# Pooled attention with a one-expert router on one core: batch 1's choice of expert, buffer counts, the first batch's order and the last batch's output blocks

## The chip, the cores and the metric

The kernel runs on one NeuronCore of a Trainium2 chip. The metric is the device time of one execution in microseconds (us), as the median of several. Engines are named as the profile has them: PE is TensorE's matmuls and PEld its weight loads, DVE is VectorE, ACT is ScalarE, POOL is GpSimd, and SP is the engine that issues the stores of the output. An L with a number is a line of the kernel before.

## The reference, cut to what matters

Attention over keys and values pooled by 8, then a cosine router that sends each token to one of eight experts, then that expert's two matmuls.

```python
# attention: q, k, v are [8 batches, 8 heads, 576 tokens, 64]
k_p = k.reshape(B, H, S // 8, 8, D).mean(axis=3)      # 72 pooled keys
v_p = v.reshape(B, H, S // 8, 8, D).mean(axis=3)
attn = softmax(q @ k_p.T / sqrt(D))
x = (attn @ v_p)                                      # as [4608 tokens, 512]
# router and experts: expert_emb [8, 512], w1 [8, 512, 1024], w2 [8, 1024, 512]
logits = normalized(x) @ normalized(expert_emb).T / tau
expert_idx = argmax(logits, axis=1)
gate_w = softmax(logits)[arange(N), expert_idx]
for e in range(8):
    mask = expert_idx == e
    h = maximum(x[mask] @ w1[e], 0)
    out[mask] = gate_w[mask, None] * (h @ w2[e])
```

## The kernel before

Work is staged by batch, 576 tokens each, in four blocks of 128 tokens and a short one of 64. Attention of batch b pools k and v (`pool_kv`, L185, matmuls in L151), transposes q (`qtr`, L192) and the pooled keys (`kpt`, L204), computes each head's scores and their exp (`score`, L219, exp on ACT in L236, one `at` tile of 16 buffers each), multiplies with the pooled values (`pv`, L240, one call a block; DVE divides into `x_sb`, L256 and L258), and transposes x (`xtr`, L263; the copy to `xt_all` is DVE, L276 and L278). `route` (L285) computes router logits, their maximum and a one-hot row per token; `count` (L308) sums these rows over the tokens, and `expert` (L315) takes the most frequent expert, reads its number into a register of POOL and has POOL issue the loads of its weights (`load_w`, L90, three buffers). In batch 0 the choice is made from block 0 alone, the other blocks are routed later, and `recount` (L336) records which experts occur in the whole batch. In the other batches all five blocks are routed and counted ahead of the choice. A loop at the kernel's end (L639) makes a further pass for every pair of a batch and an occurring expert that wasn't the chosen one.

The expert's part (`ffn_steps`, L430) has eight `hgrp` steps (eight W1 matmuls each, L442, with a ReLU on ACT in even steps, L449, and on DVE in odd ones, L451), eight `yblk` steps (four W2 matmuls each, L460; blocks 0 and 1, then 2 and 3, share a PSUM tile and are evicted together with the gate factor, the even one on DVE, L472, the odd one on ACT, L470) and `ylast` (L476) for the short block, evicted half by DVE (L488) and half by ACT (L490). Each block goes to a `y_sb` tile (four buffers, L66), and SP issues its two stores (L515). Where two engines read one PSUM tile, the second starts when the first is done. All PSUM tiles come from one ring of four (L67).

Every engine works in the order in which the program emits its instructions, and that order is written out by hand. Each step has a cost, and a step's place in its batch is its share of the summed costs. The main loop (L614) emits the expert steps of batch b and, ahead of each, all attention and gate steps whose place lies below `lead` (L610) of it: some 1.5 to 1.7 batches ahead. The gate steps of `gate_steps` (L396: `norm`, a power on POOL; `prob`, three DVE operations and an exp on ACT; `gate`, five DVE operations) have places of their own (L607).

```python
# attn_steps, b == 0: the head of the first batch (L349 to L362)
step(0.65)(lambda h=h: score(h, (12, 4, 4, 4, 10, 4, 4, 4)[h]))
# main: the rest of batch 0, interleaved with the first steps of batch 1 (L601)
for f in [s1[0], tail[0], s1[1], tail[1], tail[2], s1[2], s1[3], tail[3],
          tail[4], s1[4], tail[5], tail[6], s1[5], tail[7], s1[6], tail[8],
          s1[7], tail[9]]:
    f()
```

In the first batch nothing else is there for TensorE, and `fill` (L129) puts matmuls on a constant between the steps; their number is the second argument of `score`, `xtr`, `route` and `expert`. `head` is emitted first, then `tail` (here `pv(1)` and on) interleaved with the first eight steps of batch 1 (`s1`). The inputs come by POOL's queue: batch 0 in pieces (L530 to L544), batch 1 at L576, batch 2 at the end of the head, and batch b + 2 right after the choice of batch b (L341, L393); `kv` and `qq` have three buffers.

Of the kernel before, what the change touches and what calls it, by code (L numbers as in the profile page):

```python
# [27 lines left out]
def kernel(  # L28
# [30 lines left out]
    wpool = ctx.enter_context(tc.tile_pool(name="wpool", bufs=3))  # L59
    inp = ctx.enter_context(tc.tile_pool(name="inp", bufs=3))  # L60
    att = ctx.enter_context(tc.tile_pool(name="att", bufs=2))
    atp = ctx.enter_context(tc.tile_pool(name="atp", bufs=16))
    xp = ctx.enter_context(tc.tile_pool(name="xp", bufs=3))
    rt = ctx.enter_context(tc.tile_pool(name="rt", bufs=2))
    hp_ = ctx.enter_context(tc.tile_pool(name="hp", bufs=2))
    yp = ctx.enter_context(tc.tile_pool(name="yp", bufs=4))  # L66
    ps = ctx.enter_context(tc.tile_pool(name="ps", bufs=4, space=bass.MemoryType.PSUM))  # L67

    def psum():
# [66 lines left out]
    def attn_steps(b):  # L136
# [178 lines left out]
        def expert(cs, nfill=0):  # L315

            pc = psum()
            fill(pc[:, 512:704], nfill)
            count(cs, pc)
            mx = rt.tile([128, E], FP32, name="mx")  # L320
            nc.vector.max(out=mx, in_=pc[:, 0:E])
            ix = rt.tile([1, E], U32, name="ix")
            nc.vector.max_index(out=ix, in_max=mx[0:1], in_values=pc[0:1, 0:E])
            nc.vector.tensor_scalar(out=eb_all[:, b], in0=pc[:, 0:E], scalar1=mx[:, 0:1],
                                    scalar2=None, op0=ALU.is_ge)
            if len(cs) == NC:
                present(pc)
            e_val = nc.values_load(ix[0:1, 0:1], engines=[ENG.Pool], min_val=0,
                                   max_val=E - 1)
            weights[b] = load_w(e_val)  # L330

        def present(pc):
            nc.vector.tensor_scalar(out=pos_all[:, b], in0=pc[0:1, 0:E], scalar1=0.5,
                                    scalar2=None, op0=ALU.is_ge)

# [2 lines left out]
            count(list(range(NC)), pc)  # L338
            present(pc)

        def next_load():  # L341
            if b + 2 < B:
                load_qkv(b + 2)

        routes[b] = st
        P = lambda c: step(0.9)(lambda: pv(c))
        X = lambda c: step(0.6 if c < 4 else 1.2)(lambda: xtr(c))
        if b == 0:
            for grp in range(2):  # L349
                step(0.5)(lambda grp=grp: pool_k(grp))  # L350
                step(0.5)(lambda grp=grp: qtr(grp))
                step(0.5)(lambda grp=grp: kpt(2 * grp, 2))
                for h in range(4 * grp, 4 * grp + 4):
                    step(0.65)(lambda h=h: score(h, (12, 4, 4, 4, 10, 4, 4, 4)[h]))
                    if h == 5:
                        step(1.0)(pool_v)
            step(0.3)(lambda: emb_transposed(8))
            P(0)
            step(0.6)(lambda: xtr(0, 14))
            step(0.4)(lambda: route(0, 1, 8))  # L360
            step(0.4)(lambda: expert([0], 12))
            step(0.0)(lambda: load_qkv(2))  # L362
            head, steps = steps, []
            P(1)
            P(2)
            X(1)
            P(3)
            X(2)
            P(4)
            X(3)  # L370
            X(4)
            step(0.8)(lambda: route(1, 4))
            step(0.4)(recount)
            return head, steps
# [7 lines left out]
        P(1)  # L382
        X(0)
        P(2)
        X(1)
        P(3)
        X(2)
        P(4)
        X(3)
        X(4)  # L390
        step(1.0)(lambda: route(0, NC))
        step(0.4)(lambda: expert(list(range(NC))))
        step(0.0)(next_load)  # L393
        return steps

    def gate_steps(b):  # L396
# [30 lines left out]
        return [norm, prob, gate]  # L427


    def ffn_steps(xt, get_w, get_gm, finish):  # L430
        st = {}
        steps = []

# [19 lines left out]

        def yblk(c, part):
            w2 = get_w()[1]
            if part == 0 and c % 2 == 0:
                st['y'] = psum()
            py = st['y'][:, ts(c % 2, 512)]
            for w in range(4 * part, 4 * part + 4):
                nc.tensor.matmul(out=py,  # L460
                                 lhsT=st['hT'][:, w // 2, w % 2, ts(c, 128)],
                                 rhs=w2[:, w // 2, w % 2, :],
                                 start=(w == 0), stop=(w == 7))
            if part == 1 and c % 2:
                for i in (c - 1, c):
                    y_sb = yp.tile([128, DM], FP32, name="y_sb")
                    py = st['y'][:, ts(i % 2, 512)]
                    g = get_gm()[:, i:i + 1]
                    if i % 2:
                        nc.scalar.activation(out=y_sb, in_=py, func=AF.Copy, scale=g)  # L470
                    else:
                        nc.vector.tensor_scalar(out=y_sb, in0=py, scalar1=g, scalar2=None,  # L472
                                                op0=ALU.mult)
                    finish(i, y_sb)

        def ylast():  # L476
            w2 = get_w()[1]
# [15 lines left out]

        for w in range(8):
            steps.append((1.0, lambda w=w: hgrp(w)))
        for c in range(4):
            for part in range(2):
                steps.append((0.87, lambda c=c, part=part: yblk(c, part)))
        steps.append((0.87, ylast))
        return steps  # L500

    def out_rows(o_b, c, y_sb):
# [7 lines left out]
    def store(b):  # L510
        o_b = out[ts(b, S)]

        def finish(c, y_sb):
            for dst, src in out_rows(o_b, c, y_sb):
                nc.sync.dma_start(out=dst, in_=src)  # L515
        return finish


# [9 lines left out]
    with tc.manual_schedule():  # L528
# [61 lines left out]
        for b in range(B):  # L590
# [7 lines left out]
            if b == 1:  # L598

                s1 = [f for _, f in astream]  # L600
                for f in [s1[0], tail[0], s1[1], tail[1], tail[2], s1[2], s1[3], tail[3],  # L601
                          tail[4], s1[4], tail[5], tail[6], s1[5], tail[7], s1[6], tail[8],
                          s1[7], tail[9]]:
                    f()
                astream = astream[8:]
            for i, f in enumerate(gate_steps(b)):
                gstream.append((b + LEAD + 0.05 + 0.12 * i, f))  # L607
        astream = sorted(astream + gstream, key=lambda s: s[0])

        def lead(pos):  # L610
            return pos + LEAD - 0.2 * max(0.0, 1.0 - pos)

        j = 0
        for b in range(B):  # L614
            steps = ffn_steps(lambda b=b: xt_all[:, b], lambda b=b: weights[b],
                              lambda b=b: gates[b], store(b))
            total = sum(c for c, _ in steps)
            done = 0.0
            for c, f in steps:
                while j < len(astream) and astream[j][0] < lead(b + done / total):  # L620
                    astream[j][1]()
                    j += 1
                f()
                done += c
# [14 lines left out]
    with tc.For_i(0, n_val, 1) as i:  # L639
        f_val = nc.values_load(ext_i[0:1, ds(i, 1)], min_val=0, max_val=1)  # L640
        with tc.If(f_val > 0):
            b_val = nc.values_load(pair_b[0:1, ds(i, 1)], min_val=0, max_val=B - 1)
            e_val = nc.values_load(pair_e[0:1, ds(i, 1)], min_val=0, max_val=E - 1)
            wx = load_w(e_val)
            xt_c = att.tile([128, 4, S], FP16, name="xt_c", bufs=1)
            nc.vector.tensor_copy(
                out=xt_c, in_=xt_all[:, ds(b_val, 1), :, 0:S].squeeze(1))
            gmx = rt.tile([128, NC], FP32, name="gm")
# [6 lines left out]
            o_b = out[ds(b_val * S, S)]  # L655

            def finish(c, y_sb):
                o_sb = yp.tile([128, DM], FP32, name="o_sb", bufs=1)
                cols = DM if c < 4 else DM // 2
                for src, dst in out_rows(o_b, c, o_sb):  # L660
                    nc.sync.dma_start(out=dst, in_=src)
# [42 lines left out]
```

## Time and profile before

| what | before |
|---|---|
| median of 3 runs | 247.66 us (246.61 to 249.81) |
| profiled execution, its own time | 246.23 us |
| its span, first to last instruction | 244.6 us |
| PE busy | 218.2 us (89%) |
| PEld busy | 140.7 us (58%) |
| DVE busy | 128.1 us (52%) |
| ACT busy | 108.9 us (45%) |
| POOL busy | 42.9 us (18%) |
| mean granted TensorE clock | 0.965 of full speed |
| bytes moved by DMA, mean rate | 40.79 MB, 167 GB/s |

The span lies within the execution's own time, and 1.6 us are around it. Busy time of PE is that of pipelined matmuls whose ends are modelled: an engine that is shown as busy is not always at its peak. The granted clock has two levels here, full (1.00, 2.4 GHz) and half (0.50, 1.2 GHz). The DMA share of a window can pass 1.

### The profile page before, as it was taken

The page shows a single profiled execution, that of the slowest core. Times are in us where ns is not written, and L with a number is a line of the kernel's source. Part 1 is how long each engine was busy: PE and PEld are TensorE (multiplying, and loading weights), DVE is VectorE, ACT ScalarE, POOL GpSimd, SP SyncE. Part 2 cuts the span into 40 slices and gives each one's busy share as a digit, 9 for nine tenths or more (in the row PEclk, how much of TensorE's full clock was granted, in tenths as well). Part 3 has the DMA queues.
Part 4 walks back from the last instruction along what each step waited for, and adds up shares of the span by engine and source line. Part 5 has one row for each costly group of instructions (what it writes and reads, how often), then busy time and mean ns, then how long its engine had stood idle before and what let it go on. Part 6 is the DMA issues. An engine that isn't in the chain of part 4 may idle for free. (4 is left out here: it accounts for less than half of the span.)

```text
span 244.6 us, 5695 instructions
## 1 busy us (share of the span) xinstructions
PE 218.2 (89%) x2282; PEld 140.7 (58%) x2283; DVE 128.1 (52%) x370; ACT 108.9 (45%) x230; POOL 42.9 (18%) x61
## 2 busy tenths in 40 slices
PE   7799789999898996999899998999899999996940
PEld 2578557763676455664677366745666478465520
DVE  3224756852784356761786258535766288216220
ACT  3442483518273535537362647353553664214210
POOL 7400610070006100070007000530012000300000
PEclk9999957999999999999999999999999999999995
DMA  5996699659998999489995999599969941896061
GB/s 77 199 207 104 115 211 207 107 81 205 222 250 138 211 203 258 97 152 209 228 239 90 211 215 258 96 205 196 266 132 175 228 104 34 148 210 181 3 154 46
DMA packets 27597, 40.79 MB, mean 167 GB/s; under 512 B 1960, under 2 KB 15272, under 8 KB 27568
## 3 DMA queue, kind: packets, MB, share of 16 engines
q0 software_dynamic: 21152, 30.94, 73.2%
q1 hardware_dynamic: 6416, 9.46, 13.0%
q8 instruction: 19, 0.31, 0.5%
q14 instruction: 10, 0.08, 0.1%
HBM read 61.88 MB, written 9.44 MB: 292 GB/s over the span
## 5 line engine op out<-in xcount | busy, mean ns | idle before, releaser
L442 PE MATMUL pa<-xt_all,w 128*128 128x288 f16 x512 | 72.7, 290 | 2.6 <-ACT y_sb L490 2.5
L460 PE MATMUL pa<-w,hT 128*128 128x512 f16 x256 | 62.9, 380 | 0.0
L442 PEld LDWEIGHTS <-w 128*128 128x128 f16 x512 | 47.4, 99 | 17.0 <-issue 5.3
L236 ACT ACTIVATE at<-pa 72x576 f16<-72x576 f32 x64 | 38.1, 643 | 26.0 <-PE pa L230 25.8
L460 PEld LDWEIGHTS <-hT 128*128 128x128 f16 x256 | 21.9, 98 | 25.5 <-issue 5.6
L93 POOL DMA_DIRECT2D w<-in_moe_w_dram x8 | 6.3, 791 | 160.5 <-DVE vpx L169 121.9
L449 ACT ACTIVATE hT<-pa 128x576 f16<-128x576 f32 x32 | 20.7, 651 | 28.2 <-PE pa L442 28.0
L258 DVE TENSOR_TENSOR x_sb<-pa,r 128x512 f16<-128x512 f32 x40 | 27.7, 692 | 2.6
L472 DVE TENSOR_SCALAR y_sb<-pa,gm 128x512 f32<-128x512 f32 x16 | 12.0, 751 | 32.4 <-PE pa L460 32.4
L470 ACT ACTIVATE y_sb<-pa,gm 128x512 f32<-128x512 f32 x16 | 11.0, 688 | 37.4 <-DVE y_sb L472 37.4
L451 DVE TENSOR_SCALAR hT<-pa 128x576 f16<-128x576 f32 x32 | 24.1, 754 | 5.7 <-PE pa L442 5.4
L282 ACT ACTIVATE sq<-x_sb 128x512 f16<-128x512 f16 x40 | 25.0, 625 | 4.5 <-DVE x_sb L258 4.1
L249 PE MATMUL pa<-vpx,at 72*128 72x65 f16 (+1 forms) x384 | 19.2, 199 | 2.9 <-ACT at L236 1.2
L249 PEld LDWEIGHTS <-at 72*128 72x128 f16 (+1 forms) x384 | 16.3, 105 | 9.3 <-issue 3.0
L271 PE MATMUL pa<-ident_h,x_sb 128*128 128x128 f16 (+1 forms) x160 | 14.7, 217 | 6.8 <-DVE xt_all L276 4.9
L151 PE MATMUL pa<-kv,pmat 64*72 64x512 f16 (+2 forms) x180 | 17.5, 336 | 0.7 <-DMA kv<-in_v_dram 0.7
L230 PE MATMUL pa<-qT,kpT 64*72 64x320 f16 (+1 forms) x128 | 17.0, 316 | 0.7 <-ACT at L236 0.2
L271 PEld LDWEIGHTS <-x_sb 128*128 128x128 f16 (+1 forms) x160 | 10.6, 98 | 12.0 <-issue 7.1
L256 DVE RECIPROCAL r<-pa 128x8 f32<-128x8 f32 x40 | 8.1, 202 | 17.8 <-PE pa L249 17.7
L201 DVE COPY qT<-pa 128x1152 f16<-128x1152 f16 x16 | 12.0, 752 | 9.1 <-PE pa L199 9.1
L276 DVE COPY xt_all<-pa 128x512 f16<-128x512 f16 x32 | 13.3, 415 | 2.2 <-PE pa L271 2.0
L230 PEld LDWEIGHTS <-kpT 64*72 64x72 f16 x128 | 5.7, 112 | 12.8 <-issue 9.8
(95 smaller groups left out, 196.8 us busy)
## 6 DMA issues: line engine op xcount, KB each, us to landing
w<-in_moe_w_dram POOLq DMA_DIRECT2D x16, 1024.0 KB, 10.6
out_dram<-y_sb SPq DMA_DIRECT2D x64, 128.0 KB, 6.0
kv<-in_v_dram POOLq DMA_DIRECT2D x8, 576.0 KB, 19.4
kv<-in_k_dram POOLq DMA_DIRECT2D x7, 576.0 KB, 16.6
qq<-in_q_dram POOLq DMA_DIRECT2D x7, 576.0 KB, 23.0
out_dram<-y_sb SPq DMA_DIRECT2D x16, 64.0 KB, 5.6
kv<-in_k_dram POOLq DMA_DIRECT2D x2, 288.0 KB, 4.9
qq<-in_q_dram POOLq DMA_DIRECT2D x2, 288.0 KB, 5.7
```

What stands on the lines that cost most here:

```text
L151: nc.tensor.matmul(out=pk[0:G, par * 512 + c0:par * 512 + c0 + na * nh * D], lhsT=pmat[rows, t, :], rhs=kv[rows, a0:a0 + na, h0:h0 + nh, t ...
L230: nc.tensor.matmul(out=pS[0:G, c0:c0 + nb * 64].rearrange("g (t p) -> g t p", p=64), lhsT=st['kpT', h, half], rhs=qT[rows, blk, ts(h2, 64) ...
L236: nc.scalar.activation(out=at, in_=pS[0:G, 512 - 320:512 + 256], func=AF.Exp, scale=escale)
L249: nc.tensor.matmul(out=px[rows, h * 128:h * 128 + D + 1], lhsT=st['at', h][:, c * 128:c * 128 + L], rhs=st['vpx'][:, h // 2, h % 2, :], st ...
L258: nc.vector.tensor_tensor(out=x_sb, in0=pxv[:, :, 0:D], in1=r.unsqueeze(2).to_broadcast([128, H, D]), op=ALU.mult)
L271: nc.tensor.transpose(out=pt[:, w * 128:w * 128 + L], in_=xf[0:L, ts(w, 128)], identity=ident_h[:L, :L])
L276: nc.vector.tensor_copy(out=xt_all[:, b, :, ts(c, 128)], in_=ptv)
L282: nc.scalar.activation(out=sq, in_=xf, func=AF.Square, accum_out=st['ssq'][:, c:c + 1])
L442: nc.tensor.matmul(out=ph[:, half * 512:half * 512 + HALF], lhsT=w1v[:, kk, w // 2, w % 2, :], rhs=xt()[:, kk, ts(half, HALF)], start=(kk ...
L449: nc.scalar.activation(out=dst, in_=src, func=AF.Relu)
L451: nc.vector.tensor_scalar(out=dst, in0=src, scalar1=0.0, scalar2=None, op0=ALU.max)
L460: nc.tensor.matmul(out=py, lhsT=st['hT'][:, w // 2, w % 2, ts(c, 128)], rhs=w2[:, w // 2, w % 2, :], start=(w == 0), stop=(w == 7))
```

## The change

Batch 1, too, chooses its expert from block 0 alone: `route(0, 1)` and `expert([0])` stand between its x blocks, the other blocks are routed afterwards, and `recount` follows. The loads of batch b + 2 are issued in `expert` itself. `y_sb` has eight buffers instead of four, and `at` twelve instead of sixteen. The head of the first batch is a new list: the second pair of key heads is pooled between the scores of the first heads, most steps have fewer fills, and `pv(1)` comes ahead of the choice; `xtr(1)` gets six fills. The list that interleaves batches 0 and 1 has one entry less. `norm` gets the place b + 1.0, `prob` b + 1.82 for b + 1.87, and `gate` b + 1.94 for b + 1.99. The new expression of `lead` has the same values as the old one at every place. In the last batch (`apart`) the short block comes ahead of the other blocks, each of these has a PSUM tile and an eviction of its own, and the second of each block's two stores is issued by ACT instead of SP. The loop at the end takes its tiles from other pools.

```diff
-    atp = ctx.enter_context(tc.tile_pool(name="atp", bufs=16))
+    atp = ctx.enter_context(tc.tile_pool(name="atp", bufs=12))
-    yp = ctx.enter_context(tc.tile_pool(name="yp", bufs=4))
+    yp = ctx.enter_context(tc.tile_pool(name="yp", bufs=8))
...
             weights[b] = load_w(e_val)
+            if b + 2 < B:
+                load_qkv(b + 2)
...
         if b == 0:
-            for grp in range(2):
-                step(0.5)(lambda grp=grp: pool_k(grp))
-                step(0.5)(lambda grp=grp: qtr(grp))
-                step(0.5)(lambda grp=grp: kpt(2 * grp, 2))
-                for h in range(4 * grp, 4 * grp + 4):
-                    step(0.65)(lambda h=h: score(h, (12, 4, 4, 4, 10, 4, 4, 4)[h]))
-                    if h == 5:
-                        step(1.0)(pool_v)
-            step(0.3)(lambda: emb_transposed(8))
-            P(0)
-            step(0.6)(lambda: xtr(0, 14))
-            step(0.4)(lambda: route(0, 1, 8))
-            step(0.4)(lambda: expert([0], 12))
-            step(0.0)(lambda: load_qkv(2))
+            for f in [lambda: pool_k(0), lambda: qtr(0), lambda: kpt(0, 2),
+                      lambda: score(0, 12), lambda: score(1, 2), lambda: pool_k(1),
+                      lambda: score(2, 2), lambda: qtr(1), lambda: score(3),
+                      lambda: kpt(2, 2), lambda: score(4, 4), lambda: score(5, 4),
+                      lambda: pool_v(), lambda: score(6, 2), lambda: score(7, 4),
+                      lambda: emb_transposed(6), lambda: pv(0), lambda: xtr(0, 14),
+                      lambda: route(0, 1, 8), lambda: pv(1), lambda: expert([0], 8)]:
+                step(1.0)(f)
             head, steps = steps, []
-            P(1)
             P(2)
-            X(1)
+            step(0.6)(lambda: xtr(1, 6))
...
         P(2)
+        if b == 1:
+            step(0.3)(lambda: route(0, 1))
         X(1)
+        if b == 1:
+            step(0.3)(lambda: expert([0]))
...
-        step(1.0)(lambda: route(0, NC))
-        step(0.4)(lambda: expert(list(range(NC))))
-        step(0.0)(next_load)
+        if b == 1:
+            step(0.8)(lambda: route(1, 4))
+            step(0.3)(recount)
+        else:
+            step(1.0)(lambda: route(0, NC))
+            step(0.4)(lambda: expert(list(range(NC))))
...
-            if part == 0 and c % 2 == 0:
+            if part == 0 and (apart or c % 2 == 0):
                 st['y'] = psum()
...
-            if part == 1 and c % 2:
-                for i in (c - 1, c):
+            if part == 0 or (c % 2 == 0 and not apart):
+                return
+            for i in ((c,) if apart else (c - 1, c)):
...
+        steps += [(0.87, ylast)] + ysteps if apart else ysteps + [(0.87, ylast)]
...
-                nc.sync.dma_start(out=dst, in_=src)
+            for i, (dst, src) in enumerate(out_rows(o_b, c, y_sb)):
+                (nc.scalar if b == B - 1 and i else nc.sync).dma_start(out=dst, in_=src)
...
-                for f in [s1[0], tail[0], s1[1], tail[1], tail[2], s1[2], s1[3], tail[3],
-                          tail[4], s1[4], tail[5], tail[6], s1[5], tail[7], s1[6], tail[8],
-                          s1[7], tail[9]]:
+                for f in [s1[0], tail[0], s1[1], tail[1], s1[2], s1[3], tail[2],
+                          tail[3], s1[4], tail[4], tail[5], s1[5], tail[6], s1[6], tail[7],
+                          s1[7], tail[8]]:
...
-                gstream.append((b + LEAD + 0.05 + 0.12 * i, f))
+                gstream.append((b + (1.0, LEAD + 0.12, LEAD + 0.24)[i], f))
```

## Rows read from the trace of the kernel before

**Rows 1.** The page: TensorE's clock in 40 slices, and the W1 matmuls' group

```profile
PEclk9999957999999999999999999999999999999995
...
L442 PE MATMUL pa<-xt_all,w 128*128 128x288 f16 x512 | 72.7, 290 | 2.6 <-ACT y_sb L490 2.5
```

**Rows 2.** Windows, one batch: length, busy us of PE, PEld, DVE, ACT, POOL; clock, DMA share, GB/s

```profile
171.89:198.34 26.45, 25.09 (x271) 16.01 (x269) 15.42 (x44) 13.27 (x29) 2.76 (x3) 1.00 0.90 184
```

**Rows 3.** Waits over the span: us in total, times, longest us

```profile
DVE y_sb L488 <- DMA out_dram<-y_sb: 7.6, 3, 4.7
...
PE pa L271 <- DVE xt_all L276: 4.9, 5, 1.6
PE pa L442 <- ACT y_sb L490: 2.5, 1, 2.5
...
PE pa L151 <- DMA kv<-in_v_dram: 0.7, 1, 0.7
```

**Rows 4.** Timeline, batch 1's short block: start, length, engine; idle time before and its releaser

```profile
87.13 1.33 SPq L515 DMA_DIRECT2D out_dram<-y_sb  x1
...
92.27 1.14 PE L442 MATMUL pa<-xt_all,w 128*128 128x288 f16 x8
...
94.45 0.48 DVE L488 TENSOR_SCALAR y_sb<-pa,gm 64x256 f32<-64x256 f32 x1 [1.87 <-DMA out_dram<-y_sb]
...
95.31 0.38 PE L271 MATMUL pa<-ident_h,x_sb 128*128 128x128 f16 x4 [1.64 <-DVE xt_all L276]
...
95.54 1.14 PE L442 MATMUL pa<-xt_all,w 128*128 128x288 f16 x8
```

**Rows 5.** DMA issues at 87.1 to 87.2: KB each, us from issue to landing

```profile
out_dram<-y_sb SPq DMA_DIRECT2D x1, 128.0 KB, 7.2
```

**Rows 6.** Timeline, batch 5's short block: two W1 groups in a row

```profile
198.34 1.14 PE L442 MATMUL pa<-xt_all,w 128*128 128x288 f16 x8
...
199.80 1.14 PE L442 MATMUL pa<-xt_all,w 128*128 128x288 f16 x8
```

**Rows 7.** DMA issues at 105.3 to 106: v of batch 5

```profile
kv<-in_v_dram POOLq DMA_DIRECT2D x1, 576.0 KB, 20.5
```

**Rows 8.** Timeline: the issue of that load, and its first reader

```profile
105.69 0.77 POOL L87 DMA_DIRECT2D kv<-in_v_dram  x1
...
127.90 1.27 PE L151 MATMUL pa<-kv,pmat 64*72 64x512 f16 x10
```

**Rows 9.** Timeline, batch 3's third W1 group, last x block and `prob` (L405)

```profile
124.07 0.69 DVE L258 TENSOR_TENSOR x_sb<-pa,r 128x512 f16<-128x512 f32 x1
...
124.84 0.65 ACT L449 ACTIVATE hT<-pa 128x576 f16<-128x576 f32 x1 [1.01 <-PE pa L442]
...
125.74 0.16 DVE L405 TENSOR_SCALAR rn<-ssq 128x5 f32<-128x5 f32 x1
...
126.17 0.18 PE L289 MATMUL pa<-tie_l,ones_m 128*128 128x40 f16 x1
```

**Rows 10.** Timeline in the first batch: fourteen fills, and batch 0's first W1 group

```profile
19.55 1.32 PE L132 MATMUL pa<-ones_m 128*128 128x192 f16 x14
...
36.48 2.11 PE L442 MATMUL pa<-xt_all,w 128*128 128x288 f16 x8
```

**Rows 11.** Windows in the first batch, columns as in rows 2

```profile
25.00:30.00 5.00, 3.59 (x62) 2.80 (x61) 4.15 (x9) 2.13 (x6) 3.71 (x5) 0.95 0.73 116
35.00:40.00 5.00, 4.67 (x38) 3.11 (x37) 2.02 (x7) 2.64 (x6) 0.51 (x1) 0.52 1.17 209
```

**Rows 12.** Timeline, the end: last matmuls, last large eviction on ACT, last store

```profile
234.03 1.06 PE L482 MATMUL pa<-w,hT 128*64 128x256 f16 x16
...
234.97 0.69 ACT L470 ACTIVATE y_sb<-pa,gm 128x512 f32<-128x512 f32 x1 [2.82 <-DVE y_sb L472]
...
238.96 0.55 SPq L515 DMA_DIRECT2D out_dram<-y_sb  x1
```

**Rows 13.** DMA issues at 231.4 to 231.9: the first store of the last batch

```profile
out_dram<-y_sb SPq DMA_DIRECT2D x1, 128.0 KB, 2.2
```

More of the change, by code (lines that the diff above doesn't have):

```diff
@@ L339, in recount @@
             present(pc)
-        def next_load():
-            if b + 2 < B:
-                load_qkv(b + 2)
         routes[b] = st
@@ L427, in gate_steps, with ffn_steps @@
         return [norm, prob, gate]
-    def ffn_steps(xt, get_w, get_gm, finish):
+    def ffn_steps(xt, get_w, get_gm, finish, apart=False):
         st = {}
@@ L463, in yblk @@
                                  start=(w == 0), stop=(w == 7))
-            if part == 1 and c % 2:
-                for i in (c - 1, c):
[L466 to L474, printed above, removed]
+            if part == 0 or (c % 2 == 0 and not apart):
+                return
+            for i in ((c,) if apart else (c - 1, c)):
+                y_sb = yp.tile([128, DM], FP32, name="y_sb")
+                py = st['y'][:, ts(i % 2, 512)]
+                g = get_gm()[:, i:i + 1]
+                if i % 2:
+                    nc.scalar.activation(out=y_sb, in_=py, func=AF.Copy, scale=g)
+                else:
+                    nc.vector.tensor_scalar(out=y_sb, in0=py, scalar1=g, scalar2=None,
+                                            op0=ALU.mult)
+                finish(i, y_sb)
         def ylast():
@@ L495, in ffn_steps @@
             steps.append((1.0, lambda w=w: hgrp(w)))
[L496 to L499, printed above, removed]
+        ysteps = [(0.87, lambda c=c, part=part: yblk(c, part))
+                  for c in range(4) for part in range(2)]
+        steps += [(0.87, ylast)] + ysteps if apart else ysteps + [(0.87, ylast)]
         return steps
@@ L513, in finish @@
         def finish(c, y_sb):
-            for dst, src in out_rows(o_b, c, y_sb):
-                nc.sync.dma_start(out=dst, in_=src)
+            for i, (dst, src) in enumerate(out_rows(o_b, c, y_sb)):
+                (nc.scalar if b == B - 1 and i else nc.sync).dma_start(out=dst, in_=src)
         return finish
@@ L606 @@
             for i, f in enumerate(gate_steps(b)):
-                gstream.append((b + LEAD + 0.05 + 0.12 * i, f))
+                gstream.append((b + (1.0, LEAD + 0.12, LEAD + 0.24)[i], f))
         astream = sorted(astream + gstream, key=lambda s: s[0])
         def lead(pos):
-            return pos + LEAD - 0.2 * max(0.0, 1.0 - pos)
+            return pos + min(1.5 + 0.2 * pos, LEAD)
         j = 0
@@ L615 @@
             steps = ffn_steps(lambda b=b: xt_all[:, b], lambda b=b: weights[b],
-                              lambda b=b: gates[b], store(b))
+                              lambda b=b: gates[b], store(b), b == B - 1)
             total = sum(c for c, _ in steps)
@@ L644 @@
             wx = load_w(e_val)
-            xt_c = att.tile([128, 4, S], FP16, name="xt_c", bufs=1)
+            xt_c = inp.tile([128, 2, HP, T * D], FP16, name="kv")[:, 0]
             nc.vector.tensor_copy(
@@ L657, in finish @@
             def finish(c, y_sb):
-                o_sb = yp.tile([128, DM], FP32, name="o_sb", bufs=1)
+                o_sb = yp.tile([128, DM], FP32, name="y_sb")
                 cols = DM if c < 4 else DM // 2
```

## The prediction, written before the kernel was changed

> **What bounds the kernel now.** I read the page first: by the table above TensorE is busy for 218.2 of 244.6 us, and the next, VectorE, for 52%; the row of TensorE's clock shows one dent inside the run, in the sixth and seventh of 40 slices [rows 1]. So only time in which TensorE stands still, or runs slowly, can be won. A window cut from one batch's first W1 matmul to the next one's comes second: it lasts 26.45 us and holds 25.09 us of TensorE work at full clock [rows 2]. Something over a microsecond is lost once a batch. The list of waits names it [rows 3]: `DVE y_sb L488 <- DMA out_dram` (7.6 us, 3 times), and behind them TensorE itself, 4.9 us in five waits for `xt_all` and 2.5 us in one for L490. The timeline shows the chain [rows 4]: L488, the eviction of half of a batch's fifth output block, stands in VectorE's order ahead of the copy of a transposed x block. VectorE idles 1.87 us before it, and it starts at 94.45. The store issued at 87.13 [rows 4] took 7.2 us to land [rows 5], at 94.33: with four `y_sb` buffers the fifth block takes the first one's and waits for its store. TensorE's next transpose then waits 1.64 us for VectorE. The control is in the same trace: when the loads are over, the same piece runs without a wait, and W1 group follows W1 group in 1.46 us (198.34 to 199.80) where it took 3.27 us (92.27 to 95.54) [rows 4, 6].
>
> **Eight output buffers.** A block then takes the buffer of eight blocks earlier, well over a batch old: no store is that late. TensorE's waits of 4.9 and 2.5 us go [rows 3]. The ends of matmuls are modelled, so an interval shrinks by a little more than its idle time: in the batch shown by 3.27 - 1.46 = 1.81 us against 1.64. With 0.17 us more for each of five, 4.9 + 0.85 + 2.5 = 8.2 us. Bounds: 0 if something else holds L488, and 8.2. What is late next is the loads. The v of batch 5 is issued at 105.69 and takes 20.5 us [rows 7, 8], so it is there at 126.2, and its reader starts at 127.90 [rows 8]: 1.7 us of slack, of which about 1 us goes with the wait. It holds, narrowly. I take 8.2.
>
> **Twelve score buffers for sixteen.** A score tile then takes one of the batch before (or of the one before that), whose last reader, the `pv` of its last block, stands ahead of it in TensorE's own order. Cost 0; were it wrong, up to one x block's chain a batch, under a microsecond.
>
> **Gate steps earlier.** `prob` moves from behind batch b+1's last transposes to ahead of the third W1 group, and so ahead of that group's ReLU in ScalarE's order. In the trace x_sb ends at 124.76, the ReLU runs from 124.84, `prob` on VectorE only from 125.74, and TensorE asks for the ReLU's PSUM buffer with the router's matmuls at 126.17 [rows 9]. In the new order `prob`'s three VectorE operations (0.2 us each) run at 124.76 to 125.36; its exp (0.3) then stands before the ReLU (0.65), which ends near 126.35. The router waits 0.2 us. Six batches at 0.2 us are 1.2 us lost; bounds 0 (the exp finds room) and 6 x 0.65 = 3.9 (a whole ReLU). I take 1.2. `norm` earlier on POOL stays between the same two groups of loads, cost 0. `gate`, now ahead of the expert's count, delays the next weights by 0.2 to 0.6 us, free while the slack above lasts. `load_qkv` inside `expert` keeps its place in POOL's order, 0.
>
> **Batch 1's expert from 128 tokens.** It adds one router pass and one count: three VectorE operations and three small matmuls, about 0.6 us, and puts the choice's four operations (another 0.6) ahead of batch 1's later x blocks. In return W(1) and the inputs of batch 3 are asked for several W1 groups sooner, so the one wait of TensorE for such a load, 0.7 us [rows 3], goes. The added 1.2 us are counted with the first batch.
>
> **First batch.** There are 22 fewer fill matmuls before batch 1's pooling (66 for 88); 14 of them took 1.32 us [rows 10], so 2.1 us; `pv(1)` moves in, 0.4 us. Part of the fills only stood in waits for exps, so I take 1.3 us for the head (0 to 1.7). Then comes the interleave of two batches. Here VectorE is nearly full (4.15 of 5 us) and TensorE is not (3.59), and the granted clock falls to 0.5, the lower of its two levels, 1.2 GHz; it rises again near 39.8 (0.52 for 35 to 40) [rows 11]. `pv(1)`'s two VectorE operations (0.9 us) leave this stretch for one where VectorE has room. So 1.3 + 0.9 - 1.2 = 1.0 us. The low clock costs only where TensorE is the bound, from 36.5 on, where a W1 group takes 2.11 us [rows 10] against 1.14 [rows 4]: 3.3 x (1 - 1.14/2.11) = 1.5 us. Since the stretch keeps its holes I count none of it back. Bounds for all this: -1.5 to +3.
>
> The Trainium skill (TensorE: Matmul & The Clock Gate, "A second HAM failure mode: psum-queue depth-cycling") says that TensorE's many small idle gaps between groups of matmuls can bring the clock down, and not one long wait alone. The trace agrees: the dent follows the stretch with 3.59 of 5 us busy. By that rule the new interleave, paced by VectorE in the same way, is dented again and the sum stays; if it were not, 1.5 us would be added.
>
> **The end.** SP still has stores to issue after TensorE's last matmuls, which end at 235.1: its last goes out at 238.96 [rows 12], lands by the nearest row 2.2 us later [rows 13], at 241.2, and 3.4 us of winding down follow. With the short block first and each block in its own PSUM tile, the last eviction is one ScalarE operation of 0.69 us [rows 12] behind TensorE's last matmul, which shifts by 0.15 us since the short block needs the last ReLU sooner: 235.25 + 0.05 + 0.7 = 236.0. Its two stores are issued by SP and ScalarE side by side and land at 238.2 to 238.3. That is 2.9 us. No row shows ScalarE issuing a store; if it takes a microsecond longer than SP's 0.55 [rows 12], 1.8 us.
>
> The Trainium skill (DMA: Bandwidth & Descriptors, "Issuing engines are not separate DMA queues") says that a second issuing engine saves the sequencer's time alone. By that, ScalarE's part of the 2.9 is one issue of about 0.55 us, and the rest belongs to the blocks on their own.
>
> **Sum.** 8.2 + 0.7 - 1.2 + 1.0 + 2.9 = 11.6 us. Against the profiled execution (246.23 us: the span of 244.6 and 1.6 around it) that is 234.6. The median of the runs shown, 247.66, stands 1.4 us above the profiled one, and I let the new kernel's do the same: 236.0 us.
>
> **Rivals.**
> A: the loads become the bound, and `PE L151 <- DMA kv` takes the place of L488. For: the 1.7 us of slack, and `gate` delaying the next weights. Against: the DMA share is 0.90 over the batch of [rows 2] and 1.17 at its fullest [rows 11], so a batch's traffic needs 26.45 x 0.90/1.17 = 20 us. Then batches keep their length and only batch 6's 2.5, the end's 2.9 and the front's 1.0 are left: 247.66 - 6.4 = 241.3.
> B: the earlier `prob` and the added choice cost their upper ends: 3.9 for 1.2, and nothing from the front. 236.0 + 3.7 = 239.7. For: ScalarE and VectorE have little room around the third W1 group.
> C: the change doesn't do what it says, since L488 waits for something other than its buffer: the list puts only three of its waits down to the store. 236.0 + 8.2 = 244.2. Against: 94.33 beside 94.45, and the control.
> S, slower: thinner fills and the holes of the interleave keep the clock at its lower level far into batch 0's expert. At 2.11 us for 1.14, each us of dense work costs 0.85 more, so 11.6 us are gone after 13.6 us of it, which is if the clock rises only about 65 us into the span instead of at 39.8: then 248, and 250 a few us on. Against: it rose after 3.3 us of dense matmuls.
> No rival is a second pass with another expert's weights for batch 1: the page's 512 W1 matmuls [rows 1] are eight batches of 64, so every token of a batch goes to that batch's expert, the first 128 too.
>
> **Chances.** Forecast 0.65 (its own range 233 to 239), A 0.12, B 0.12, C 0.07, S 0.04. Two per cent is 5 us, about what this measurement can tell from no change: faster means below 242.7. The forecast, B and nearly all of A lie there: 0.87; C and the rest of A give 0.09; S 0.04. The range leaves out C, S and the ends of the others: 232.5 to 242.
>
> **What would show it.** Right: no idle time of L488 before `out_dram`, no wait of L271 for `xt_all` over 0.3 us, 25.3 to 25.7 us from one batch's first W1 matmul to the next one's, the last store landing 3.1 us after the last matmul, batch 2's pooling about 1 us sooner. Wrong: `PE L151 <- DMA kv` once a batch (A); the router's first matmul L289 waiting over 0.3 us for ScalarE's hT (B); L488 still idle a microsecond and more (C); more than three low slices in the row of the clock (S).

## The result, and the profile after

| | before | after |
|---|---|---|
| median, beside each other on one chip | 248.74 us (4 runs) | 233.22 us (4 runs, 231.71 to 234.87) |
| profiled execution, its own time | 246.23 us | 231.71 us |
| its span | 244.6 us | 230.1 us |
| PE busy | 218.2 us (89%) | 214.9 us (93%) |

The ratio is 0.940 (95% interval 0.928 to 0.953): faster. Two repeats in other sessions gave 0.939 (0.931 to 0.947) and 0.939 (0.933 to 0.945). The forecast was 236.0 us, range 232.5 to 242. The sum was 2.9 us short, 11.6 us for 14.5 in the profiled executions, and the sections below look for the difference, term by term.

Cut at the first W1 matmul of each batch, the two spans compare so (us; the last column is the forecast's own term for that stretch):

| stretch | before | after | change | forecast |
|---|---|---|---|---|
| start to batch 1's pooling | 22.89 | 21.31 | -1.58 | -1.3 |
| from there to batch 0's first W1 | 13.59 | 12.09 | -1.50 | -0.9 |
| batch 0 | 28.73 | 29.45 | +0.73 | +1.2 |
| batches 1 to 5 together | 133.13 | 126.07 | -7.07 | -5.3 |
| batch 6 | 18.21 | 18.33 | +0.12 | 0 |
| batch 7, to its last matmul | 18.55 | 16.18 | -2.37 | -2.4 |
| from there to the span's end | 9.47 | 6.67 | -2.80 | -3.0 |

The page's row of the clock and the W1 group, to be held against [rows 1]:

```profile
PEclk9999988999999999999999999999999999999997
...
L441 PE MATMUL pa<-xt_all,w 128*128 128x288 f16 x512 | 72.3, 289 | 0.0
```

The 2.5 us of idle time ahead of that group are gone (lines have moved up by one: L442 is L441). One batch as a window, for [rows 2]:

```profile
163.71:188.92 25.21, 24.95 (x270) 15.93 (x268) 15.14 (x44) 13.26 (x29) 2.74 (x3) 1.00 0.93 194
```

25.21 us for 26.45, and a quarter of a microsecond without TensorE work. All five batches from 1 to 5 have this length to 0.01 us. In the list of waits [rows 3] no row puts L488 down to a store, and none L271 to `xt_all` or L151 to a load. What is left of them, and the longest wait of TensorE for a load:

```profile
DVE y_sb L488 <- PE pa L482: 0.6, 2, 0.4
...
PE pa L199 <- DMA qq<-in_q_dram: 1.4, 1, 1.4
```

The short block's chain of [rows 4], for the same batch (batch 1's output, at batch 2's start):

```profile
88.07 1.14 PE L441 MATMUL pa<-xt_all,w 128*128 128x288 f16 x8
88.30 0.47 DVE L488 TENSOR_SCALAR y_sb<-pa,gm 64x256 f32<-64x256 f32 x1
...
88.69 0.41 DVE L276 COPY xt_all<-pa 128x512 f16<-128x512 f16 x1
...
89.31 0.39 PE L271 MATMUL pa<-ident_h,x_sb 128*128 128x128 f16 x4
...
89.53 1.14 PE L441 MATMUL pa<-xt_all,w 128*128 128x288 f16 x8
```

L488 and the transposes have no bracket now, and the second W1 group follows the first after 1.46 us, the value of the control [rows 6], where it took 3.27.

The surroundings of `prob`, for [rows 9]:

```profile
116.94 0.69 DVE L258 TENSOR_TENSOR x_sb<-pa,r 128x512 f16<-128x512 f32 x1
...
117.55 0.16 DVE L404 TENSOR_SCALAR rn<-ssq 128x5 f32<-128x5 f32 x1
...
118.21 0.33 ACT L411 ACTIVATE lg<-lg,lnxs 128x40 f32<-128x40 f32 x1 [1.69 <-DVE lg L408]
...
118.44 0.63 ACT L448 ACTIVATE hT<-pa 128x576 f16<-128x576 f32 x1
...
118.90 0.18 PE L289 MATMUL pa<-tie_l,ones_m 128*128 128x40 f16 x1
```

The exp (L411) does stand ahead of the ReLU (L448), as forecast. But the router's matmul L289 starts at 118.90, in the middle of the ReLU, which runs until 119.07: it doesn't take the ReLU's PSUM buffer.

The first batch, windows for [rows 11] and then the first W1 group for [rows 10]:

```profile
25.00:30.00 5.00, 3.58 (x58) 2.48 (x57) 4.83 (x12) 3.20 (x8) 2.31 (x4) 1.00 1.05 180
30.00:35.00 5.00, 4.13 (x50) 2.73 (x50) 2.14 (x8) 3.30 (x8) 1.20 (x1) 0.78 1.12 211
35.00:40.00 5.00, 4.63 (x60) 3.68 (x58) 3.56 (x12) 2.59 (x7) 0.00 (x0) 0.88 1.19 207
```

```profile
33.40 2.11 PE L441 MATMUL pa<-xt_all,w 128*128 128x288 f16 x8
```

The dent of the clock is there again, behind the same stretch in which VectorE is full (4.83 of 5 us) and TensorE is not, and the first W1 group falls into it. Here it lasts 3.4 us; in the two repeats it lasted 6.8, in the kernel before 10.2.

The end, for [rows 12], and the landing of ScalarE's last store as the view of DMA issues has it:

```profile
222.52 2.13 SPq L514 DMA_DIRECT2D out_dram<-y_sb  x2
222.53 0.50 ACTq L514 DMA_DIRECT2D out_dram<-y_sb  x1
223.47 0.69 ACT L470 ACTIVATE y_sb<-pa,gm 128x512 f32<-128x512 f32 x1 [2.77 <-PE pa L459]
224.19 0.50 ACTq L514 DMA_DIRECT2D out_dram<-y_sb  x1
```

```profile
out_dram<-y_sb ACTq DMA_DIRECT2D x1, 128.0 KB, 2.6
```

TensorE's last matmul ends at 223.43 and the last eviction follows it at once. ScalarE's last store lands 2.6 us after its issue at 224.19, at 226.8: 3.4 us after that matmul, where 3.1 were forecast from the 2.2 us of a store of SP [rows 13].

### The profile page after: what moved, and what is told of

It is laid out like the page before. It is cut to its first block, busy times and chain, and to the rows that moved or that the text cites. A ratio compares the mean times of both kernels' runs of the same rounds, so it can differ in the third digit from the quotient of the medians.

```text
span 230.1 us, 5654 instructions
## 1 busy us (share of the span) xinstructions
PE 214.9 (93%) x2269; PEld 138.3 (60%) x2270; DVE 126.9 (55%) x373; ACT 108.7 (47%) x230; POOL 42.8 (19%) x61
## 4 chain that ended last, share of the span: by engine, by line
PE 66%; ACT 10%; DMA 10%; DVE 9%; issue 1%; POOL 1%; POOLq 0%; DVEq 0%
PE pa L441 22%; PE pa L459 18%; DMA out_dram<-y_sb 8%; PE pa L151 7%; ACT at L236 4%; PE pa L230 4%; PE pa L199 3%; PE pa L132 3%; PE pa L249 3%; ACT sq L282 2%; DVE y_sb L472 2%; DMA qq<-in_q_dram 2%; PE pa L271 2%; DVE x_sb L258 2%; PE pa L482 2%; ACT hT L448 2%
## 5 line engine op out<-in xcount | busy, mean ns | idle before, releaser
L441 PE MATMUL pa<-xt_all,w 128*128 128x288 f16 x512 | 72.3, 289 | 0.0
L441 PEld LDWEIGHTS <-w 128*128 128x128 f16 x512 | 47.3, 99 | 14.1 <-issue 2.5
L448 ACT ACTIVATE hT<-pa 128x576 f16<-128x576 f32 x32 | 20.7, 647 | 18.8 <-PE pa L441 18.6
L151 PE MATMUL pa<-kv,pmat 64*72 64x512 f16 (+2 forms) x180 | 17.5, 336 | 0.0
L230 PE MATMUL pa<-qT,kpT 64*72 64x320 f16 (+1 forms) x128 | 16.0, 298 | 1.3 <-ACT at L236 0.6
L271 PE MATMUL pa<-ident_h,x_sb 128*128 128x128 f16 (+1 forms) x160 | 14.6, 214 | 0.6 <-ACT at L236 0.6
L170 DVE CAST vpx<-pa 72x512 f16<-72x512 f32 x8 | 5.5, 690 | 16.6 <-ACT kp L164 14.5
```

The lines of the kernel that those rows point to most:

```text
L151: nc.tensor.matmul(out=pk[0:G, par * 512 + c0:par * 512 + c0 + na * nh * D], lhsT=pmat[rows, t, :], rhs=kv[rows, a0:a0 + na, h0:h0 + nh, t ...
L230: nc.tensor.matmul(out=pS[0:G, c0:c0 + nb * 64].rearrange("g (t p) -> g t p", p=64), lhsT=st['kpT', h, half], rhs=qT[rows, blk, ts(h2, 64) ...
L271: nc.tensor.transpose(out=pt[:, w * 128:w * 128 + L], in_=xf[0:L, ts(w, 128)], identity=ident_h[:L, :L])
L441: nc.tensor.matmul(out=ph[:, half * 512:half * 512 + HALF], lhsT=w1v[:, kk, w // 2, w % 2, :], rhs=xt()[:, kk, ts(half, HALF)], start=(kk ...
L448: nc.scalar.activation(out=dst, in_=src, func=AF.Relu)
```

## The experiments

Each kernel was timed in three rounds beside the kernel before (247.93 us in the first group of runs, 247.67 in the second, 248.66 in the third). One caution on the medians: executions differ by 1 to 2.5 us in the first batch, for a reason found at the end of this section. Where a part is worth less than that, the stretch of the trace decides and not the median.

**The output buffers, taken back.**

```diff
-    yp = ctx.enter_context(tc.tile_pool(name="yp", bufs=8))
+    yp = ctx.enter_context(tc.tile_pool(name="yp", bufs=4))
```

> The new kernel with four y_sb buffers again, all else new. Theory (the fifth block waits for the first block's store): the idle time of VectorE before L488 comes back, TensorE's interval from a batch's first W1 group to the second goes from 1.47 us back to 2.3 to 3.3 us, batches take about 26 to 27 us instead of 25.2, and the kernel loses 7 to 9 us (some 241 us). Rival (the waits had another source, and one of the other parts removed them): less than 2 us lost, intervals stay at 1.47 us.

Measured: 241.78 us, ratio 0.974 (0.970 to 0.979), as the theory had it. Rows of its list of waits:

```profile
DVE y_sb L488 <- DMA out_dram<-y_sb: 9.4, 5, 3.8
...
PE pa L271 <- DVE xt_all L276: 4.7, 4, 1.6
...
PE pa L441 <- ACT y_sb L490: 1.5, 1, 1.5
```

The waits of [rows 3] are back, in batches 2 to 5 and in the last; those batches take 26.5 to 27.1 us and the second W1 group comes 2.63 to 3.24 us after the first. Batch 2, say, loses 26.53 - 25.21 = 1.32 us, of which 1.19 are its longer interval between the two groups: the buffers give another 0.13 us a batch that isn't in this wait.

**The output buffers alone.** The kernel before with eight (and `at` with twelve and the loop at the end changed as in the change, for the space).

```diff
-    atp = ctx.enter_context(tc.tile_pool(name="atp", bufs=16))
+    atp = ctx.enter_context(tc.tile_pool(name="atp", bufs=12))
-    yp = ctx.enter_context(tc.tile_pool(name="yp", bufs=4))
+    yp = ctx.enter_context(tc.tile_pool(name="yp", bufs=8))
```

> The old kernel with eight y_sb buffers (and twelve score buffers, to make room), all else old. Theory: VectorE's idle time before L488 goes, batches take 25.2 to 25.3 us, except the one with TensorE's wait for the load of v, and the kernel gains 8.2 to 9 us of the 15, some 239 us. Rival (the loads or another wait take over once the stores are out of the way): batches of 25.6 us and more, under 6 us gained.

Measured: 241.34 us, ratio 0.972 (0.965 to 0.979), 6.3 us less than the kernel before beside it. No row of L488 for a store or of L271 for `xt_all` is left, and batches 2 to 5 take 25.21 or 25.22 us. The gain stays below the theory's 8.2 to 9 us. What is late instead is batch 3's v, in batch 1:

```profile
PE pa L151 <- DMA kv<-in_v_dram: 1.7, 1, 1.7
```

```profile
75.76 3.82 PE L151 MATMUL pa<-kv,pmat 64*72 64x512 f16 x18 [1.73 <-DMA kv<-in_v_dram]
```

That wait was 0.7 us [rows 3]. TensorE is ready a microsecond sooner and the load isn't: rival A in small, for one batch of five. And the clock is low behind the wait (0.66 for 75 to 80 us): the pooling takes 3.82 us where it takes 2.13 in the kernel before, and batch 1 takes 28.71 us for 27.07.

**Batch 1's choice from all blocks.** All five blocks are routed and counted ahead of batch 1's choice, as in the other batches.

```diff
-        if b == 1:
-            step(0.3)(lambda: route(0, 1))
...
-        if b == 1:
-            step(0.3)(lambda: expert([0]))
...
+        step(1.0)(lambda: route(0, NC))
+        step(0.4)(lambda: expert(list(range(NC))))
```

> The new kernel, but batch 1 chooses its expert from all five blocks, as before. Theory (the early choice costs 0.7 to 1.2 us in the first batch and saves 0.7 us, TensorE's wait for the load of v of batch 3): the stretch from batch 0's first W1 matmul to batch 1's first one gets 0.7 to 1.2 us shorter, and TensorE's wait for v (L151) comes back with 0.3 to 1.5 us, so the run changes by less than 1 us. Rival (the early choice is a plain gain): the stretch keeps its length and the kernel loses 0.7 us or more. Rival 2: a plain loss, the wait does not come back and the kernel gains about 1 us.

Measured: 235.95 us (234.46 to 238.29), ratio 0.954 (0.948 to 0.961). The timeline of TensorE has the wait again:

```profile
72.30 1.05 PE L151 MATMUL pa<-kv,pmat 64*72 64x512 f16 x8 [1.52 <-DMA kv<-in_v_dram]
```

Batch 0 takes 28.86 us and batch 1 26.81, together 55.67; the new kernel's first repeat, with a dent of the same 6.8 us, has 29.69 + 25.22 = 54.91. So the early choice costs 0.8 us of added work in batch 0, saves 1.6 in batch 1, and is worth 0.8, close to the theory. The rest of the difference of the medians isn't its own: 0.8 us of it is a later landing of the last store, told in the last section.

**The gate steps at their old places.**

```diff
-                gstream.append((b + (1.0, LEAD + 0.12, LEAD + 0.24)[i], f))
+                gstream.append((b + LEAD + 0.05 + 0.12 * i, f))
```

> The new kernel with the gate steps at their old places (norm b + 1.75, prob b + 1.87, gate b + 1.99). The prediction's step (prob ahead of the third W1 group costs the router 0.2 us a batch): batches become shorter, 25.0 us instead of 25.2, and the kernel gains 1.2 us. Theory now (the router's matmuls take a buffer that VectorE frees, so the earlier prob costs nothing and saves a wait): batches of 25.3 us, a loss of 0.5 us over the run. Rival: no difference in the length of a batch, within 0.03 us, and the 0.12 us a batch below the old 25.33 us came with something else.

Measured: 239.13 us, ratio 0.962 (0.955 to 0.970). Both theories missed and the rival's equal batches came: batches 1 to 5 keep their 25.21 us, so `prob`'s place neither costs nor gives anything there. But batch 0 takes 35.41 us for 29.69, which no expectation had. The timeline of POOL, and what waits for it:

```profile
44.24 0.75 POOL L93 DMA_DIRECT2D w<-in_moe_w_dram  x1 [14.46 <-DVE x_sb L258]
...
47.17 0.79 POOL L88 DMA_DIRECT2D qq<-in_q_dram  x1
47.93 1.27 POOL L400 TENSOR_TENSOR ssq<-ssq,half_c 128x5 f32<-128x5 f32 x1
49.23 0.17 DVE L404 TENSOR_SCALAR rn<-ssq 128x5 f32<-128x5 f32 x1 [2.96 <-POOL ssq L400]
...
50.91 0.27 PE L293 MATMUL pa<-enT,xt_all 128*128 128x8 f16 x4 [3.66 <-DVE xt_all L278]
```

`norm` of batch 0 stands behind the five loads that batch 1's choice makes POOL issue, at 0.75 to 0.79 us each. `prob`, its reader, stands in VectorE's order ahead of the copy of batch 1's last x block (L278), and the router of TensorE waits 3.66 us for that copy. A second stretch at the lower clock follows, from 49.6 to 56.5 us. In the new kernel `norm` stands at b + 1.0, ahead of these loads, and VectorE doesn't wait for it.

**The first batch's order, taken back.** The old list of the head, the old numbers of fills and the old interleave.

```diff
-                      lambda: score(0, 12), lambda: score(1, 2), lambda: pool_k(1),
...
+                    step(0.65)(lambda h=h: score(h, (12, 4, 4, 4, 10, 4, 4, 4)[h]))
...
-                for f in [s1[0], tail[0], s1[1], tail[1], s1[2], s1[3], tail[2],
+                for f in [s1[0], tail[0], s1[1], tail[1], tail[2], s1[2], s1[3], tail[3],
```

> The new kernel with the first batch's head and the list that interleaves it with batch 1 as before, all else new. Theory (the new order is worth some 3 us up to batch 0's first W1 matmul: 1.6 us of fills ahead of batch 1's pooling and 1.5 us of VectorE work moved out of the stretch that VectorE paces): first W1 matmul at about 36.5 us at equal clock, 2 to 3.5 us lost. Rival (most of the 3 us were the shorter low-clock stretch, which changes from execution to execution): first W1 matmul at 34 to 35 us in a profile whose low-clock stretch is as short as the new kernel's, 3.4 us, and less than 1.5 us lost over the executions.

Measured: 238.02 us, ratio 0.960 (0.956 to 0.966). Batch 0's first W1 comes at 37.88, and at 35.38 and 35.55 in two kernels with the new order whose clock was low in the same stretches and for as long (the four-buffer one and the second repeat): 2.3 to 2.5 us. Batch 0 itself takes 30.18 us, for 29.7 to 30.0. The new order is worth 2.5 to 3 us. (Another 1.1 us of this kernel's time is the later end of the last section: 7.76 us from the last matmul, for 6.66.)

**The old end.** No separate tiles and no short block first; all stores by SP.

```diff
-                               lambda b=b: gates[b], store(b), b == B - 1)
+                               lambda b=b: gates[b], store(b))
```

> The new kernel with the last batch as before: blocks in pairs, short block last, all stores by SP. Theory (the prediction's step: 2.9 us): 9.5 us from the last matmul to the end instead of 6.7, and the run 2.5 to 3 us longer. Rival (the end is set by the landing of the last store and the winding down alone): under 1 us.

Measured: 235.71 us, ratio 0.950 (0.942 to 0.959). From the last matmul to the end it takes 8.58 us for 6.67, and the last batch reaches that matmul 0.27 us sooner: the new end is worth 1.6 us, between the theory's 2.5 to 3 and the rival's less than 1.

**The stores of the new end all by SP.**

```diff
-                (nc.scalar if b == B - 1 and i else nc.sync).dma_start(out=dst, in_=src)
+                nc.sync.dma_start(out=dst, in_=src)
```

> The new kernel with each block of the last batch on its own, but all stores issued by SP. By the rule that a second issuing engine saves the sequencer's time alone: 0.5 to 0.6 us more from the last matmul to the end than with ScalarE's help, 7.2 to 7.3 us. Rival (ScalarE's issues are slower or wait longer than SP's): no difference, or SP alone is ahead.

Measured: 235.24 us, ratio 0.947 (0.940 to 0.954). From the last matmul to the end: 7.27 us for 6.68, so ScalarE's part is 0.59 us, one issue. (The rest of the median's difference is its first batch, whose first W1 came at 37.03.) The Trainium skill (DMA: Bandwidth & Descriptors, "Issuing engines are not separate DMA queues") says that a second issuing engine saves no more than the sequencer's time; the trace agrees, 0.59 us.

**Fills where TensorE waits.** In the profiles above the first batch varied. Where TensorE waited 2.0 us and more for the first load of q, it ran at the lower clock right behind in all profiles but one, and in those batch 1's pooling came 1.5 us and more late on top of the wait. And the dent near 30 us had three lengths. The second repeat shows the first of these in its timeline of TensorE:

```profile
8.34 1.14 PE L199 MATMUL pa<-ident_h,qq 128*128 128x128 f16 x9 [2.22 <-DMA qq<-in_q_dram]
...
9.53 2.11 PE L132 MATMUL pa<-ones_m 128*128 128x192 f16 x12
```

Twelve fills take 1.16 us at full clock. So fills were put into the new kernel, ahead of the first transposes of q, into the interleave, and into both; the second repeat of the new kernel ran beside them.

```diff
+            fill(pq[:, 512:704], nfill)
...
-            for f in [lambda: pool_k(0), lambda: qtr(0), lambda: kpt(0, 2),
+            for f in [lambda: pool_k(0), lambda: qtr(0, 16), lambda: kpt(0, 2),
```

> The new kernel with sixteen fills ahead of the first batch's first transposes of q, in the time in which TensorE waits 1.4 to 2.3 us for that load. Theory (TensorE is clocked down in its first microseconds in those executions in which that wait is long, and this makes the spread of the runs): the steps behind the wait run at full clock in every execution, ten fills of 192 columns and two more take 1.16 us and not 2.12, batch 1's pooling starts between 21 and 22.5 us, and the median is 0.5 to 1.5 us below the new kernel's beside it. Rival (the clock in that stretch doesn't hang on that wait): the front is as before, and the fills cost 0 to 0.8 us, since they begin late and the transposes stand behind them.

```diff
-            X(2)
+            step(0.6)(lambda: xtr(2, 6))
             P(4)
-            X(3)
-            X(4)
-            step(0.8)(lambda: route(1, 4))
+            step(0.6)(lambda: xtr(3, 6))
+            step(1.2)(lambda: xtr(4, 6))
+            step(0.8)(lambda: route(1, 4, 6))
```

> The new kernel with six fills each ahead of the first batch's third, fourth and fifth transposes of x and its second router pass, in the stretch in which VectorE sets the pace and TensorE has holes. Theory (these holes bring the low clock that follows): the stretch of low clock near 30 to 36 us, 3.4 or 6.8 us long, is gone, batch 0's first W1 group takes 1.14 us and not 2.11, and batch 0 is 1 to 2.5 us shorter, 27.5 to 28.5 us. Rival (the clock falls for another reason, or the fills stand in TensorE's way): the low stretch stays and the 24 fills cost 0 to 2 us, so that the first W1 group comes as much later.

> The new kernel with both sets of fills. If both theories hold, the sum of both: 1.5 to 4 us below the new kernel beside it, about 229.5 us. If neither holds, 0 to 2.8 us above it.

> The new kernel again, beside these: 232 to 235 us. By the theory of the first loads its runs lie in two groups, with batch 1's pooling at 21 to 22.5 us or 23.5 to 25 us, by how long TensorE waits for the first load of q.

| | median | range | batch 1's pooling | to batch 0's W1 | batch 0 | last matmul to end |
|---|---|---|---|---|---|---|
| new kernel, second repeat | 233.40 | 232.32 to 234.05 | 23.46 | 12.09 | 29.72 | 6.66 |
| fills ahead of q | 233.83 | 233.37 to 234.62 | 21.59 | 12.39 | 30.37 | 7.68 |
| fills in the interleave | 234.07 | 232.66 to 234.89 | 23.94 | 12.96 | 28.11 | 7.68 |
| both | 233.17 | 232.97 to 233.40 | 21.89 | 12.96 | 28.11 | 7.67 |

The first microseconds of the kernel with fills ahead of q, then the page's row of the clock for the second repeat, the fills ahead of q, those in the interleave, and both.

```profile
6.03 1.50 PE L132 MATMUL pa<-ones_m 128*128 128x192 f16 x16
7.96 0.68 PE L201 MATMUL pa<-ident_h,qq 128*128 128x128 f16 x9 [0.43 <-DMA qq<-in_q_dram]
...
8.61 1.16 PE L132 MATMUL pa<-ones_m 128*128 128x192 f16 x12
```

```profile
PEclk9799976999999999999999999999999999999997
```

```profile
PEclk9999956999999999999999999999999999999995
```

```profile
PEclk9799999999999999999999999999999999999997
```

```profile
PEclk9999999999999999999999999999999999999996
```

Behind each set of fills the dent is gone: the one at 8 us, the one at 30, or both. (The one at 8 us is missing in some profiles without fills, too.) With both the row of the clock is full until the last matmul, and the four runs lie within 0.43 us, where the new kernel's spread over 1.7 to 3.2. The mean clock of the single runs agrees: 0.990 to 0.995 in these four, at most 0.987 in all twelve of the new kernel. The first W1 group then takes half the time of the one shown above:

```profile
34.84 1.15 PE L443 MATMUL pa<-xt_all,w 128*128 128x288 f16 x8
```

But the fills pay for it: those in the interleave save 1.6 us in batch 0 and cost 0.87 ahead of its first W1; those ahead of q save the 1.5 us of low clock in an execution that has it behind the wait, and next to nothing in one without. And all three kernels lost 1.0 us at their end, as told in the last section; the one with both waits another 0.4 us for the v of batch 7. Both sets together have a ratio of 0.940 (0.934 to 0.945), the new kernel beside them 0.939 (0.933 to 0.945): steadier, not faster. Of the expectations, those for the clock and for the pooling came, the medians did not.

## Why the prediction was right, and where its terms were not

**Eight output buffers: 8.2 us, right in mechanism, and in size to a microsecond.** Taken back they cost some 8.5 us by the medians (0.974 of the time before against 0.939 and 0.940) and 7.5 by the stretches (5.8 in batches 2 to 5, 1.7 in the last batch); alone they bring 6.3, since the load that becomes late when nothing else is changed takes 1.0 us and the low clock behind it 1.7. The sum missed 0.12 us a batch, 0.6 in all: the forecast counted the one interval around L488, and the batch has shrunk a little elsewhere too.

**The load of v, 0.7 us: right.** With the early choice there is no such wait; without it, and with the buffers, it is 1.5 to 1.7 us. The early choice thus covers what the faster batches would have uncovered. The 1.7 us of slack in [rows 8] held for the later batches, narrowly: only the kernel with both sets of fills waits for one of them, 0.4 us.

**`prob` earlier, -1.2 us: wrong.** The step that failed is "TensorE asks for the ReLU's PSUM buffer with the router's matmuls". It was read from the order of two times in [rows 9], the ReLU's end at 125.49 and the router's start at 126.17, and no row showed that one waits for the other. In the new order the router starts in the middle of the ReLU, and with the old place batches 1 to 5 are as long: the term is 0, the lower of its bounds. With the 0.6 above this is the 1.8 us by which batches 1 to 5 did better than forecast.

**`norm` earlier, 0: the wrong question was asked.** The forecast said that it "stays between the same two groups of loads". It does, but only because it was moved: with the early choice at its old place it stands behind five more issues of POOL, and batch 0 is 5.7 us longer (3.7 of wait, the rest at the lower clock). A move that gains nothing by itself can be the cover of another edit.

**First batch, +1.0: near in its terms, undersized in the sum.** The stretches give 1.58 + 1.50 - 0.73 = 2.35 us. The head's 1.3 was right: from the first transposes of q to batch 1's pooling 15.05 us became 13.63, 1.4 us, and the rest of the 1.58 is an earlier load. The interleave's 0.9 was right at equal dents: with one of 6.8 us that stretch takes 12.92 us in the old order and 12.09 in the new one. The other 0.7 of its 1.50 goes with the longer dent in the profile of the kernel before, 10.2 us; the forecast counted nothing back for the dent, whose length changes from profile to profile, so that part came by luck. The added work, taken as 1.2, is 0.8 by the kernel with the choice from all blocks. The Trainium skill (TensorE: Matmul & The Clock Gate, "A second HAM failure mode: psum-queue depth-cycling") says that small idle gaps of TensorE between groups of matmuls bring the clock down. The runs agree: the dent came again behind the same holes, and went when fills stood in them.

**The end, 2.9: right in sum by luck, not in its parts.** The trace has 2.80, and ScalarE's issue is 0.59 for 0.55. But the old end put into the new kernel takes 8.58 us, not 9.47: 0.9 of the 2.80 is a delay of SP's stores that the profiles of the kernel before and of the one with the buffers alone (9.53 us) have, and which the forecast took for the cost of that end.

**Twelve score buffers, 0: no wait for them appears.** They were not tried apart.

**The rivals.** A showed itself for one batch each in the kernel with the buffers alone (1.7 us), the one without the early choice (1.5) and the one with both sets of fills (0.4); C and S didn't. B fell with `prob`'s 0; an early choice that costs more than it brings is what the kernel with the old gate places has, at 239.1 us, by a wait on POOL that B didn't name.

## What to carry to other kernels

- Where a buffer is given back by a store, ask in the order of the engine that waits what stands behind the wait: here 1.9 us of VectorE for half an output block became 1.6 us of TensorE in the batch shown, and 4.9 us over five batches.
- When a choice or a load is moved forward, list all that its engine issues with it, and what on that engine now stands behind: five issues at 0.75 us each were more than the choice was worth.
- Judge a part worth a microsecond by its stretch of the trace. The medians of these variants carry the first batch's 2 us and an end's 1 us that belong to none of them.

## What the runs showed of the hardware

A wait can cost more than its own length. In the second repeat 2.2 us without work for TensorE at 6 us cost another 1.5 us at the lower clock (15.1 us from the transposes of q to batch 1's pooling, for 13.6); 1.4 and 1.6 us, in the new kernel's other two profiles, cost nothing further. The length alone doesn't decide it. These are the transposes in the kernel with the choice from all blocks and in the one with the buffers alone, the first at full clock, the second at the lower one:

```profile
8.79 0.68 PE L199 MATMUL pa<-ident_h,qq 128*128 128x128 f16 x9 [2.04 <-DMA qq<-in_q_dram]
```

```profile
7.98 1.14 PE L199 MATMUL pa<-ident_h,qq 128*128 128x128 f16 x9 [1.24 <-DMA qq<-in_q_dram]
```

What decides between the two stays open.

The end of a kernel can meet the program's own code. Ten of the profiles have the new end as it is. In five of these profiles (the new kernel three times, four output buffers, the old gate places) the span ends 6.66 to 6.69 us after the last matmul, in the other five (the choice from all blocks, the old front, the three with fills) 7.4 to 7.8 us. The view of DMA over the last stores of the kernel with both sets of fills, and the same store in the second repeat:

```profile
q8 instruction: 1, 0.02, 3.8%
...
out_dram<-y_sb ACTq DMA_DIRECT2D x1, 128.0 KB, 3.6
```

```profile
out_dram<-y_sb ACTq DMA_DIRECT2D x1, 128.0 KB, 2.6
```

In the five late ones a transfer of 16 KB of instructions occupied one of the DMA engines for 1.1 to 1.4 us between the last stores; in the five others such transfers ended over 4 us before the last store was issued or began 1.7 us and more after it had landed. In the kernel before, such a transfer lies beside an SP issue that took 1.28 us, and in the one with the buffers alone beside one of 1.37; the same issue in the old end under the new kernel took 0.59. In this order:

```profile
236.72 1.28 SPq L515 DMA_DIRECT2D out_dram<-y_sb  x1
```

```profile
231.98 1.37 SPq L515 DMA_DIRECT2D out_dram<-y_sb  x1
```

```profile
227.10 0.59 SPq L514 DMA_DIRECT2D out_dram<-y_sb  x1
```

The Trainium skill (Runtime: NRT & Kernel Launch, "Instruction fetch mechanics") says that instructions come in blocks of 16 KiB and that fetching them is mostly hidden. The size agrees; in the late profiles the fetch doesn't look hidden from the stores. That it delays them is read from these profiles, and was not tried: no run moved it alone.
